# Grouped-query decode with wo loaded in 32 KB rows and turned on VectorE

## The chip, the cores and the metric

The kernel runs on one core of one Trainium2 chip. A core has TensorE (PE, with its weight loads shown as PEld), VectorE (DVE), ScalarE (ACT), GpSimd (POOL), SyncE (SP) and sixteen DMA engines, which all run at once and wait for each other by semaphores. The metric is the device time of one execution in microseconds, as the median of several runs; lower is better.

## The reference

Two layers follow each other twice, with the same weights and the same caches both times: grouped-query attention over a cache, and a gated dense layer. There are 4 rows of 512 numbers (B = 4, one token each), 32 query heads, 8 key and value heads, 4096 cached positions, 128 numbers a head. All inputs are bfloat16.

```python
def A(x, k_cache, v_cache, wq, wo):                  # wq 512x4096, wo 4096x512
    q = (x @ wq).reshape(B, 1, 32, 128).transpose(0, 2, 1, 3)
    k = repeat(k_cache, 4, axis=1)                   # cache: 4 x 8 x 4096 x 128
    v = repeat(v_cache, 4, axis=1)
    p = softmax(einsum("bhqd,bhkd->bhqk", q, k) * 128 ** -0.5)
    o = einsum("bhqk,bhkd->bhqd", p, v)
    return o.transpose(0, 2, 1, 3).reshape(B, 1, 4096) @ wo

def F(x, w_gate, w_up, w_down):                      # 512x1792, 512x1792, 1792x512
    return (gelu(x @ w_gate) * (x @ w_up)) @ w_down

x = x + A(layernorm(x), ...)
x = x + F(layernorm(x), ...)
x = x + A(layernorm(x), ...)
x = x + F(layernorm(x), ...)
```

The K cache is 32 MiB, the V cache 32 MiB. wq and wo are 4 MiB each, the three dense weights 1.75 MiB each.

## The kernel before

The kernel takes the four rows of x one after the other. For each row b it does the first attention (L = 0), the dense layer, and the second attention (L = 1). K of a row is loaded once and used by both attentions; V is loaded for both, since it doesn't stay. The second dense layer is done once for all four rows at the end.

**Memory.** `KV` has 12 places of 8 KB per partition, each for one head of K or of V (1 MB); a head of V in the second attention often comes as two halves of 512 KB, with rows of 4 KB. `wq_sb`, `wo_sb`, `wg_sb`, `wu_sb` and `wd_sb` hold the weights all the time; the room of `wq_sb` is given to four heads of V at the very end. In `wo_sb` (128 partitions, 32 heads, 512 columns) partition d holds, for each query head, row d of that head's part of wo.

**Steps of an attention.** K comes in with positions on partitions and has to be turned: for six heads of eight VectorE does so in place, in blocks of 32x32 words of 32 bits (`turn`, L366, two instructions of 1024 words a head); for two heads PE and ScalarE do (`kturn` L373, `kcopy` L379). The scores (`scores`, L415) of four heads gather in one bank `S_ps`. VectorE takes the maximum (L421) and makes the bias (L429 to L432), ScalarE the exponential (L438), VectorE turns P in blocks (L447), PE swaps the blocks (L455), ScalarE copies the result (L463). Then come P times V (`values`, L485, 32 matmuls a head), the scaling by the sum (`oscale`, L493), and the output projection with wo (`proj`, L613; `proj_last`, L623, with `half_out` L632 and `half_sum` L639 before it). For L = 0 the projection has four parts by key and value heads: 0 to 3, 4 and 5, 6, and 7. `addback` (L646, L647) adds the result to x. The dense layer is `up` (L655), `ffturn` (L662), the gelu (L678 to L707) and `down` (L715). The next query is made by L538 to L605 and L392.

**Order of the work.** Nothing is scheduled at run time. A planner (`Plan`) knows each step as a node with an engine, a duration and what it depends on. `Plan.run` walks through an imagined execution and gives out the steps one after another; the instructions are issued in this order, engine by engine, and wait for each other by semaphores. Where two steps of one engine could go, the one with the longer way to the end goes first; `LEAD` adds some microseconds to that length by kind of step, and `PATIENCE` says how long an engine may be held back for a more pressing step. Loads stand in one fixed list (`pl.load`) and are all issued by SP in that order (x alone by ScalarE); a load of K or V waits for a place of `KV` whose last reader is done. The second figure of `pl.load` is its cost for the planner, in KB per partition.

`Plan.warm` then finds holes of PE and fills them with matmuls whose result is not used (`spin`, L1004), which keep PE busy; `WARM` and `FILL` set how many.

The list begins with x, wq, the eight heads of K of row 0, the first half of wo (16 query heads, 2 MB), the eight heads of V, the second half of wo, w_gate, w_up, w_down in two halves, then K and V of row 1. Each half of wo comes as 128 partitions times 16 rows of 1 KB (`ld_wo`, L795). A projection of L = 0 waits for the half of wo that holds its heads (`parts`).

Of the kernel before, what the change touches and what calls it, by code (L numbers as in the profile page):

```python
# [10 lines left out]
I32 = mybir.dt.int32  # L11
# [3 lines left out]
P = 128  # L15
# [15 lines left out]
DMA_FETCH = 1.5  # L31
DMA_LEAD = 4.0

PATIENCE = (0.5, 1.5, 0.7)
LEAD = {"tn1": -3, "val0": 1, "sc10": -2, "chain": 2, "sc11": -6, "sm00": 1, "os0": -6, "op": -2, "sm01": 11, "sm10": 10, "qx1": 4, "other": 5, "sc00": 2, "sm11": 8, "os1": -4, "tn0": -2, "sc01": 1}
EARLY = {("pt", 1): 60.0, ("su", 1): 60.0}
WINDOW = 3.413
WARM = 0.45
FILL = 0.7
SPIN = 0.22  # L40
STREAM = {"sc": 0.85, "qm": 0.85, "up": 0.75, "up2": 0.75, "kt": 0.21, "pw": 0.16, "qp": 0.11, "qn": 0.05,
          "su": 0.02, "lnm": 0.03, "xt": 0.1, "ys": 0.2, "dn": 0.38, "dn2": 0.38}
# [2 lines left out]
def stage(n):  # L45

    if isinstance(n, str):
        return "end"
    if n[0] in ("val", "va", "vd", "vf", "os"):
        return f"{'os' if n[0] == 'os' else 'val'}{n[2]}"  # L50
    if n[0] == "sc" or n[0] in ("mx", "bi", "ex", "pt", "pw", "pc", "su", "rc"):
        return f"{'sc' if n[0] == 'sc' else 'sm'}{n[2]}{n[3]}"
    if n[0] in ("tn", "kt", "kc"):
        return f"{'tn' if n[0] == 'tn' else 'kt'}{n[2] // 4}"
    if n[0] in ("op", "yo", "ys", "oa"):
        return "op"
    if n[0] in ("qs", "qp", "qx"):
        return f"qx{n[2]}"
    if n[0] in ("lnq", "lnm", "lnc", "lnv", "lnr", "up", "ft", "ga", "gb", "gy", "gc", "zz", "dn", "da", "qm", "qe",
                "qt", "qn", "qc", "qk"):  # L60
        return "chain"
    return "other"


class Plan:
# [7 lines left out]
    def add(self, name, eng, dur, deps, emit, acq=(), rel=(), soft=(), ins=0):  # L73
        assert name not in self.nodes, name
        self.nodes[name] = dict(eng=eng, dur=dur, deps=[d for d in deps if d is not None],
                                emit=emit, acq=acq, rel=rel, soft=list(soft), ins=ins)
        return name
# [9 lines left out]
    def levels(self):  # L87
# [6 lines left out]
        for first in nodes:  # L94
            stack = [first]
            while stack:
# [8 lines left out]
                level[m] = own + max([level[a] for a in after[m]], default=0.0)  # L105
        return {n: v + LEAD.get(stage(n), 0.0) + EARLY.get(n[:1] + n[2:3], 0.0) for n, v in level.items()}

    def run(self, slots, extra=()):
# [16 lines left out]
        while len(order) < len(nodes):  # L125
# [12 lines left out]
            for eng, c in cand.items():  # L138
                c.sort()
                s, lv, n = c[0]  # L140
                for s2, lv2, n2 in c[1:]:
                    if s2 > s + min(PATIENCE[0] * nodes[n]["dur"], PATIENCE[1]):
                        break
                    if lv2 < lv - PATIENCE[2] and s2 - c[0][0] < PATIENCE[1]:
                        s, lv, n = s2, lv2, n2
# [37 lines left out]
            else:  # L183
                ready.discard(n)
                e = s + v["dur"]
                if v["eng"] == "PE":
                    gap = min(s - free.get("PE", 0.0), 1.2 if n[0] == "val" else 99.0)
                    done += 2 * int(max(0.0, FILL * gap - 0.2) / SPIN)
                    while done > edge:
# [25 lines left out]
    def warm(self, places):  # L215
# [3 lines left out]
        for n, _ in self.order:  # L219
# [5 lines left out]
            if place:  # L225
                busy = sum(t * min(1.0, (y - (z - WINDOW)) / (y - x)) for x, y, t in past if y > z - WINDOW)
                most = 1.2 if n[0] == "val" else z - a
                k = max(int(min(most, max(0.0, FILL * (z - a) - 0.2)) / SPIN),
                        min(int(max(0.0, z - a - 0.05) / SPIN), int(max(0.0, WARM * WINDOW - busy) / SPIN + 1.0)))
                if k:  # L230
# [10 lines left out]
def kernel(  # L241
# [13 lines left out]
    nc = tc.nc  # L255
# [17 lines left out]
    wo_sb = wts.tile([P, Hq, D], BF16, name="wo_sb")  # L273
# [10 lines left out]
    def keep(shape, dt, name):  # L284
# [41 lines left out]
                            op=ALU.add)  # L326
# [410 lines left out]
    pl = Plan()  # L737
    add = pl.add

    def plain(dst, src, pat):  # L740
        return lambda pick: nc.sync.dma_start(out=dst, in_=src.rearrange(pat, q=P))  # L741

    def groups(b, L):

        g = [[0, 1, 2, 3], [4, 5], [6], [7]]
        if L:
            g = [[7], [6, 5, 4], [3, 2, 1, 0]] if b < B - 1 else [[0], [1, 2, 3], [7], [4, 5], [6]]
        return g
# [4 lines left out]
    def loads_k(b):  # L753
        for j in range(8):
            soft = []
            if b and j >= 3:
                soft = [("sc", b - 1, 1, 0 if j < 7 else 1, 1)]
            elif b:
                soft = [("val", b - 2, 1, 2 - j, 1) if b > 1 else ("val", 0, 0, 4 + j, 1)]
            pl.load(("k", b, j), 8, ld_head(("k", b, j), A_k_cache[b, j]), [("sc", b, 1, j // 4, 1)],  # L760
                    soft=soft)

    def loads_v(b, L):
        heads = [j for j in sum(groups(b, L), []) if not (L and j in HELD[b])]
        for i, j in enumerate(heads):
            halves = (b, L, j) in HALVES
            held = L == 0 and j in HELD[b]
            if L == 0:
                if j >= 4:
                    soft = [("val", b, 0, j - 4, 1)]  # L770
                elif b and j == 3 and HELD[b - 1]:
                    soft = [("val", b - 1, 1, HELD[b - 1][0], 1)]
                else:
                    soft = [("sc", b - 1, 1, 1, 1)] if b else []
                soft = [soft, soft]
            elif b == B - 1:
                soft = [[("sc", b, 1, 0, 1)]] * 2
            elif i < 3:
                soft = [[("val", b + 1, 0, 4 + i, 1)]] * 2
            else:  # L780
                soft = [[("val", b, 1, heads[i - 3], m)] for m in range(2)]
            src = A_v_cache[b, j]
            name = ("v", b, L, j)
            rd = [[("val", b, L, j, m)] + ([("val", b, 1, j, m)] if held else []) for m in range(2)]
            if halves:
                for m in range(2):
                    pl.load(name + (m,), 4.1, ld_part(name, m, src), rd[m], soft=soft[m], half=True)
            else:
                pl.load(name, 8, ld_head(name, src), rd[0] + rd[1], soft=soft[1])
# [1 line left out]
    def ld_x(pick):  # L791
        nc.scalar.dma_start(out=xr[0:16], in_=A_x.rearrange("b s (t n) -> (b s t) n", t=4))

    def ld_wo(n):
        return lambda pick: nc.sync.dma_start(  # L795
            out=wo_sb[:, 16 * n:16 * n + 16],
            in_=A_wo[2048 * n:2048 * n + 2048].rearrange("(h p) n -> p h n", p=P))

    def ld_wd(k):
        return lambda pick: nc.sync.dma_start(  # L800
# [2 lines left out]
    pl.load("x", 0.5, ld_x, None)  # L803
    pl.load("wq", 32, plain(wq_sb[:], A_wq, "(q c) n -> q c n"), None)
    loads_k(0)
    pl.load(("wo", 0), 20.5, ld_wo(0), None)
    loads_v(0, 0)
    pl.load(("wo", 1), 20.5, ld_wo(1), None)
    pl.load("wg", 14, plain(wg_sb[:], B_w_gate, "(q c) n -> q c n"), None)
    pl.load("wu", 14, plain(wu_sb[:], B_w_up, "(q c) n -> q c n"), None)  # L810
    for k in range(2):
# [32 lines left out]
    def spread_q(b, L, z, after):  # L844
        a = add(("qs", b, L, z), "DVE", 0.26, [after, ("qp", b, L, 0) if z else None],
                qsplit(z, 0 if L else b))
        p = add(("qp", b, L, z), "PE", 0.2, [a], qrep(z), acq=("T1",), ins=8)
        add(("qx", b, L, z), "DVE", 0.4, [p, ("sc", b, L, 0, 1) if z else
                                          (("sc", b, 0, 1, 1) if L else ("sc", b - 1, 1, 1, 1) if b else None)],
            expand(z), rel=("T1",))  # L850
        return a
# [16 lines left out]
    qproj("i", a, al, B, rrow, r, 0)  # L868
    pl.nodes[("qm", "i", 0)]["deps"].append("wq")

    def parts(b, L):

        g = groups(b, L)
        if L == 0:
            return [(h, [("os", b, 0, i), ("wo", h[0] // 4)]) for i, h in enumerate(g)]
        return [(h, [("os", b, 1, i)]) for i, h in enumerate(g)]

    def outproj(tag, b, L, bs, nb, after):
        pre, p = None, parts(b, L)
        whole = len(p) - (1 if L else 2)  # L880
        for k, (heads, deps) in enumerate(p[:whole]):
            pre = add(tag + (k,), "PE", 0.21 * len(heads) + 0.15, deps + [pre] + after,
                      proj(OT[L], nb, heads, k == 0, k == whole - 1), ins=8 * len(heads))
        free = [("val", b, 0, j, 1) for j in range(4)]
        for m in range(2):
            pre = add(("yo",) + tag + (m,), "ACT", 0.4, [pre] + free, half_out(m))
            pre = add(("ys",) + tag + (m,), "PE", 0.5, [pre], half_sum(m, nb), ins=8)
            free = []
        for k, (heads, deps) in enumerate(p[whole:]):
            pre = add(tag + (whole + k,), "PE", 0.21 * len(heads) + 0.15, deps + [pre] + after,  # L890
                      proj_last(OT[L], nb, heads, k == len(p) - whole - 1), ins=32 * len(heads))
        return add(("oa",) + tag, "DVE", 0.52, [pre], addback(bs, nb, 1))

    dense_end = None
    for b in range(B):
        bs = slice(b, b + 1)
        for L in range(2):
            if L == 0:
                if b:
                    q = spread_q(b, 0, 0, ("qx", b - 1, 1, 1))  # L900
# [41 lines left out]
            if L == 0:  # L942
                a = outproj(("op", b), b, 0, bs, 1, [dense_end] + was2)
                a = ln(("f", b), a, bs, 1, rs[:, 0:1])
                g = [None, None]
# [34 lines left out]
    c = add("rowz", "DVE", 0.1, [("os", B - 1, 1, i) for i in range(len(groups(B - 1, 1)))], rows_clear)  # L980
    c = add("rows", "DVE", 0.7, [a, c], rows)
    a = ln("f2", a, al, B, rs)
    g = [None, None]
# [68 lines left out]
```

## Time and profile before

| | |
|---|---|
| median of 3 runs | 292.16 us (292.12 to 294.27) |
| profiled execution | 291.89 us, of which the span of the profile is 290.1 us |
| bytes read from HBM | 111.42 MB |
| loads of K, and of V | 32 of 1 MB; 38 of 1 MB and 46 of 512 KB |
| loads of wo | 2 of 2 MB |
| granted PE clock | 0.998 |

The page gives each engine's busy time, cuts the span into 40 slices with a digit for the busy tenths of each, sums up the DMA queues, and follows back the chain of work that ended last. The windows give the same figures for stretches that one chooses: the length, then for each engine busy microseconds and the number of instructions, the granted clock, the share of time in which the sixteen DMA engines had packets under way (over 1 where packets overlap), and GB/s. In the timeline, a row has the start, the duration, the engine, the line, the operation with what it writes and reads, and in brackets how long the engine had stood idle before and what ended that. SPq are the instructions with which SP issues loads; their long durations are waits for room.

### The profile page before, as it was taken

To read this page: it belongs to the slowest core of one execution; us is meant where nothing else is said; L and a number is where in the kernel's file an instruction comes from. 1 tells how busy PE (TensorE), PEld (TensorE's weight loads), DVE (VectorE), ACT (ScalarE), POOL (GpSimd) and SP (SyncE) were. 2 spreads that over 40 slices of the span, in tenths; PEclk is the share of its full clock that TensorE was granted. 3 is DMA by queue.
4 is the path that set the end of the run, shared out by engine and by line. 5 is a ranking of instruction groups with operands and counts; after the bars stand their busy time and mean duration, and the time that the engine had idled before them with its cause. 6 is when DMAs were issued, how large, how long until landed. Compare 5 with 4: busy or idle time off the path is not lost.

```text
span 290.1 us, 9733 instructions
## 1 busy us (share of the span) xinstructions
PE 236.3 (81%) x4419; PEld 138.3 (48%) x4419; DVE 133.5 (46%) x380; ACT 74.5 (26%) x167; POOL 0.7 (0%) x6
## 2 busy tenths in 40 slices
PE   4988887878687888798888698879977889897794
PEld 1433454443233565455434465554445655565552
DVE  4149911002289942052389721343998213444034
ACT  1020751001023852101224731000338321113010
POOL 0000000000000000000000000000000000000000
PEclk9999999999999999999999999999999999999999
DMA  7999999999999999999999999999999999999910
GB/s 312 412 421 419 376 405 416 414 371 426 415 407 395 419 421 417 402 407 406 393 417 416 425 416 411 405 407 390 413 422 416 408 387 403 396 382 420 411 47 1
DMA packets 21657, 112.04 MB, mean 386 GB/s; under 512 B 2032, under 2 KB 6128, under 8 KB 12272
## 3 DMA queue, kind: packets, MB, share of 16 engines
q1 hardware_dynamic: 21568, 111.42, 95.3%
q8 instruction: 34, 0.56, 0.8%
q14 instruction: 7, 0.06, 0.0%
q10 hardware_dynamic: 48, 0.01, 0.0%
HBM read 111.42 MB, written 0.00 MB: 384 GB/s over the span
## 4 chain that ended last, share of the span: by engine, by line
DMA 62%; PE 16%; SPq 11%; DVE 7%; issue 2%; ACT 1%; DVEq 0%
DMA KV<-in_A_v_cache_dram 43%; DMA KV<-in_A_k_cache_dram 8%; SPq L351 7%; PE O_ps L485 7%; DMA wd_sb<-in_B_w_down_dram 6%; DMA wq_sb<-in_A_v_cache_dram 5%; SPq L741 3%; PE S_ps L415 3%; DVE KV L366 2%; PE R_ps L715 1%; PE R_ps L538 1%; DVE PA L662 1%; PE S_ps L1004 1%; PE R_ps L655 1%; DVE sm L421 1%
## 5 line engine op out<-in xcount | busy, mean ns | idle before, releaser
L485 PE MATMUL O_ps<-PA,KV 128*128 128x56 bf16 x1920 | 66.3, 188 | 20.8 <-DMA KV<-in_A_v_cache_dram 17.3
L485 PEld LDWEIGHTS <-KV 128*128 128x128 bf16 x1920 | 57.6, 97 | 40.8 <-DMA KV<-in_A_v_cache_dram 32.4
L1004 PE MATMUL S_ps<-iden_b 128*128 128x512 bf16 x226 | 67.7, 401 | 3.6 <-DVE iden_b L321 3.6
L366 DVE STREAM_TRANSPOSE KV<-KV 128x1024 int32<-128x1024 int32 x48 | 56.5, 1214 | 0.6 <-DMA KV<-in_A_k_cache_dram 0.4
L379 ACT ACTIVATE KV<-R_ps 128x512 bf16<-128x512 f32 x64 | 34.9, 595 | 28.0 <-PE R_ps L373 27.9
L415 PE MATMUL S_ps<-KV,PA 128*32 128x512 bf16 x384 | 35.3, 394 | 2.1 <-DVE KV L366 1.3
L1004 PEld LDWEIGHTS <-iden_b 128*128 128x128 bf16 x227 | 21.9, 107 | 27.6 <-issue 11.7
L373 PE MATMUL R_ps<-iden_b,KV 128*128 128x128 bf16 x256 | 22.1, 219 | 6.3 <-ACT KV L379 3.1
L421 DVE TENSOR_REDUCE sm<-S_ps 128x1 f32<-128x512 f32 x16 | 10.8, 677 | 27.4 <-PE S_ps L415 27.4
L373 PEld LDWEIGHTS <-KV 128*128 128x128 bf16 x256 | 15.8, 97 | 14.8 <-issue 10.2
L415 PEld LDWEIGHTS <-PA 128*32 128x32 bf16 x384 | 11.4, 94 | 13.2 <-issue 4.4
L493 DVE TENSOR_TENSOR OT<-O_ps,XS 128x4 bf16<-128x4 f32 (+1 forms) x12 | 2.0, 164 | 32.9 <-PE O_ps L485 32.9
L415 PE MATMUL S_ps<-KV,QN 128*32 128x512 bf16 x128 | 16.8, 381 | 0.2 <-ACT KV L379 0.2
L438 ACT ACTIVATE PA<-S_ps,sm 128x512 bf16<-128x512 f32 x16 | 11.7, 732 | 20.4 <-DVE sm L432 17.6
L632 ACT ACTIVATE PA<-R_ps 128x256 f32<-128x256 f32 x10 | 3.8, 384 | 46.2 <-PE R_ps L613 41.1
L529 ACT ACTIVATE sm<-sm 128x1 f32<-128x1 f32 (+1 forms) x10 | 2.0, 203 | 52.6 <-DVE sm L522 52.6
L493 DVE TENSOR_TENSOR OT<-O_ps,rdk 128x16 bf16<-128x16 f32 (+3 forms) x18 | 3.1, 170 | 26.7 <-PE O_ps L485 26.7
L463 ACT ACTIVATE PA<-T_ps 128x512 bf16<-128x512 f32 x16 | 9.6, 597 | 13.0 <-PE T_ps L455 11.8
L556 DVE STREAM_TRANSPOSE PA<-PA 128x256 int32<-128x256 int32 x10 | 4.4, 437 | 14.9 <-ACT PA L551 14.2
L613 PE MATMUL R_ps<-wo_sb,OT 128*1 128x512 bf16 (+1 forms) x124 | 8.7, 378 | 2.6 <-DMA wo_sb<-in_A_wo_dram 1.4
L646 DVE STREAM_TRANSPOSE PA<-R_ps 128x128 f32<-128x128 f32 x9 | 2.9, 317 | 16.5 <-PE R_ps L623 10.2
L447 DVE STREAM_TRANSPOSE PA<-PA 128x256 int32<-128x256 int32 x16 | 7.0, 434 | 7.5 <-ACT PA L438 7.5
(92 smaller groups left out, 173.9 us busy)
## 6 DMA issues: line engine op xcount, KB each, us to landing
KV<-in_A_v_cache_dram SPq DMA_DIRECT2D x34, 1024.0 KB, 15.0
KV<-in_A_k_cache_dram SPq DMA_DIRECT2D x32, 1024.0 KB, 13.5
KV<-in_A_v_cache_dram SPq DMA_DIRECT2D x46, 512.0 KB, 7.0
wq_sb<-in_A_wq_dram SPq DMA_DIRECT2D x1, 4096.0 KB, 12.2
wo_sb<-in_A_wo_dram SPq DMA_DIRECT2D x2, 2048.0 KB, 19.5
wq_sb<-in_A_v_cache_dram SPq DMA_DIRECT2D x4, 1024.0 KB
wg_sb<-in_B_w_gate_dram SPq DMA_DIRECT2D x1, 1792.0 KB
wu_sb<-in_B_w_up_dram SPq DMA_DIRECT2D x1, 1792.0 KB
```

What stands on the lines that cost most here:

```text
L351: nc.sync.dma_start(out=where[name], in_=src.rearrange("(p c) d -> p (c d)", p=P))
L366: nc.vector.transpose(out=w, in_=w)
L373: nc.tensor.matmul(R_ps[k % 2][:, P * u:P * u + P], lhsT=where[name][:, at:at + P], rhs=iden_b[:], start=True, stop=True)
L379: nc.scalar.activation(out=where[name][:, 512 * k:512 * k + 512], in_=R_ps[k % 2][:], func=ACT.Copy)
L415: nc.tensor.matmul(S_ps[z][32 * t:32 * t + 32], lhsT=w, rhs=k, start=(m == 0 and x == 0), stop=(m == 1 and x == 3))
L421: nc.vector.tensor_reduce(out=cms[:, z:z + 1], in_=S_ps[z][:].rearrange("p c r -> p (c r)"), axis=AX.X, op=ALU.max)
L438: nc.scalar.activation(out=PW[L][z].rearrange("p (a r e) -> p a r e", a=8, e=2), in_=S_ps[z][:].rearrange("p (a e) r -> p a r e", e=2), fu ...
L463: nc.scalar.activation(out=PW[L][z], in_=T_ps[z][:].rearrange("p t x -> p (t x)"), func=ACT.Copy)
L485: nc.tensor.matmul(Ov[L][:, j], lhsT=vw[:, c, :], rhs=w[:, c // 2, :, c % 2].unsqueeze(1).broadcast_to([P, WIDE, 4]), start=(m == 0 and c ...
L613: nc.tensor.matmul(R_ps[0][32 * i:32 * i + nb, :], lhsT=src[:, 4 * j + i, 0:nb], rhs=wo_sb[:, 4 * j + i, :], start=(first and j == heads[0 ...
L741: return lambda pick: nc.sync.dma_start(out=dst, in_=src.rearrange(pat, q=P))
L1004: nc.tensor.matmul(sinks[place].rearrange("p (a n) -> p a n", a=4), lhsT=iden_b[:], rhs=every, start=True, stop=True)
```

## The change

wo is now loaded whole, in four DMAs, right behind K of row 0 and ahead of V. DMA q fills partitions 32q to 32q + 31: partition 32q + h gets, for query head h, the rows 32q to 32q + 31 of that head's part of wo, which lie behind each other in HBM as 32 KB. So each partition holds one query head's quarter, where the projection wants one row of every head. Eight new steps on VectorE (`wo_turn`) set this right in place: each takes 32 words of 32 bits (64 columns of wo) of the 32 rows of a partition, and turns the 32x32 blocks of heads by rows. After them `wo_sb` holds what it held before. Each of the eight waits for all four DMAs, and every projection of L = 0 waits for all eight.

The planner's figures change with it: the cost of a load of wo, and `PATIENCE`, `LEAD`, `WARM` and `FILL`. Nothing else is edited; the order in which the planner gives out the steps of each engine changes with the figures.

```diff
-PATIENCE = (0.5, 1.5, 0.7)
-LEAD = {"tn1": -3, "val0": 1, "sc10": -2, "chain": 2, "sc11": -6, "sm00": 1, "os0": -6, "op": -2, "sm01": 11, "sm10": 10, "qx1": 4, "other": 5, "sc00": 2, "sm11": 8, "os1": -4, "tn0": -2, "sc01": 1}
+PATIENCE = (0.5, 1.5, 0.4)
+LEAD = {"tn1": -3, "val0": 1, "sc10": -2, "chain": 2, "sc11": -6, "sm00": 1, "os0": -7, "op": 1, "sm01": 7, "sm10": 10, "qx1": 4, "other": 2, "sc00": 2, "sm11": 6, "os1": -4, "tn0": -2, "sc01": 1, "end": -1}
...
-WARM = 0.45
-FILL = 0.7
+WARM = 0.5
+FILL = 0.8
...
-    def ld_wo(n):
+    def ld_wo(q):
         return lambda pick: nc.sync.dma_start(
-            out=wo_sb[:, 16 * n:16 * n + 16],
-            in_=A_wo[2048 * n:2048 * n + 2048].rearrange("(h p) n -> p h n", p=P))
+            out=wo_sb[32 * q:32 * q + 32].rearrange("p c n -> p (c n)"),
+            in_=A_wo.rearrange("(h q c) n -> q h (c n)", q=4, c=32)[q])
+
+    def wo_turn(k):
+        def emit():
+            w = wo_sb[:].rearrange("p c n -> p (c n)").bitcast(I32).rearrange("p (c n) -> p n c", c=32)
+            w = w[:, 32 * k:32 * k + 32]
+            nc.vector.transpose(out=w, in_=w)
+        return emit
...
     loads_k(0)
-    pl.load(("wo", 0), 20.5, ld_wo(0), None)
+    for q in range(4):
+        pl.load(("wo", q), 7.8, ld_wo(q), None)
     loads_v(0, 0)
-    pl.load(("wo", 1), 20.5, ld_wo(1), None)
...
+    wo_ready = [add(("wt", k), "DVE", 1.25, [("wo", q) for q in range(4)], wo_turn(k)) for k in range(8)]
+
     def parts(b, L):
 
         g = groups(b, L)
         if L == 0:
-            return [(h, [("os", b, 0, i), ("wo", h[0] // 4)]) for i, h in enumerate(g)]
+            return [(h, [("os", b, 0, i)] + wo_ready) for i, h in enumerate(g)]
```

## The prediction

> **What bounds the kernel now.** I read the page first: engines, slices, queues, chain.
>
> ```profile
> span 290.1 us, 9733 instructions
> PE 236.3 (81%) x4419; PEld 138.3 (48%) x4419; DVE 133.5 (46%) x380; ACT 74.5 (26%) x167; POOL 0.7 (0%) x6
> DMA  7999999999999999999999999999999999999910
> DMA packets 21657, 112.04 MB, mean 386 GB/s; under 512 B 2032, under 2 KB 6128, under 8 KB 12272
> q1 hardware_dynamic: 21568, 111.42, 95.3%
> DMA 62%; PE 16%; SPq 11%; DVE 7%; issue 2%; ACT 1%; DVEq 0%
> ```
>
> No compute engine is full. The queue that loads K, V and weights has packets under way for 95.3% of all engine time, its row of digits falls only in the last two slices, and DMA holds 62% of the chain. So the kernel is a stream of 111 MB followed by a tail. What the stream does not do at full rate is the time that can be had; the windows show where that is.
>
> ```profile
> core 0: us, PE busy (x) PEld busy (x) DVE busy (x) ACT busy (x) POOL busy (x), PEclk, DMA share, GB/s
> 2.00:12.00 10.00, 8.29 (x35) 3.03 (x36) 3.85 (x23) 0.43 (x3) 0.00 (x0) 1.00 0.92 389
> 14.00:30.00 16.00, 13.87 (x127) 5.74 (x126) 11.61 (x16) 1.63 (x4) 0.00 (x0) 1.00 1.01 421
> 30.00:40.00 10.00, 8.24 (x109) 4.99 (x101) 5.82 (x12) 8.68 (x17) 0.00 (x0) 1.00 1.06 375
> 40.00:56.00 16.00, 13.76 (x269) 8.23 (x267) 2.16 (x8) 2.46 (x5) 0.00 (x0) 1.00 1.01 419
> 56.00:66.00 10.00, 6.96 (x94) 3.67 (x94) 0.49 (x3) 0.00 (x0) 0.00 (x0) 1.00 1.08 381
> ...
> 86.00:88.00 2.00, 1.94 (x29) 0.83 (x22) 1.90 (x7) 0.18 (x1) 0.00 (x0) 1.00 0.81 324
> ...
> 254.00:256.00 2.00, 1.54 (x36) 0.85 (x28) 1.11 (x3) 0.60 (x1) 0.00 (x0) 1.00 1.00 342
> 256.00:258.00 2.00, 2.00 (x33) 0.81 (x32) 0.00 (x0) 0.00 (x0) 0.00 (x0) 1.00 1.01 350
> ...
> 274.00:276.00 2.00, 1.42 (x40) 0.99 (x37) 0.17 (x1) 0.00 (x0) 0.00 (x0) 1.00 0.97 389
> 276.00:278.00 2.00, 1.95 (x53) 1.21 (x50) 0.18 (x1) 0.03 (x1) 0.00 (x0) 1.00 0.28 104
> ```
>
> The last column is the rate. Rows of 8 KB run at 419 to 421. Two stretches of 10 us run at 375 and 381 although the engines are more than full (1.06, 1.08). SP's order of issue says that these are the halves of wo: each is issued between K and V, or between V and the dense weights.
>
> ```profile
> 15.39 0.38 SPq L795 DMA_DIRECT2D wo_sb<-in_A_wo_dram  x1
> 17.88 33.57 SPq L351 DMA_DIRECT2D KV<-in_A_v_cache_dram  x8
> 51.50 0.43 SPq L795 DMA_DIRECT2D wo_sb<-in_A_wo_dram  x1
> 51.98 8.13 SPq L741 DMA_DIRECT2D wg_sb<-in_B_w_gate_dram  x1
> ```
>
> wo is 4 MiB (4.19 MB) in rows of 1 KB, so 4096 of the 6128 packets under 2 KB. Data stops about 276.5; 13.6 us of PE and VectorE work follow, which this edit leaves as it is.
>
> **The change, part by part.**
>
> *wo's rows.* 4096 rows of 1 KB become 128 rows of 32 KB, 32 in each of four DMAs. At 420 GB/s the bytes of the two slow stretches would have taken 10 × (375 + 381) / 420 = 18.0 us, not 20.0. Lost to the short rows: 2.0 us; wo therefore costs 4.19 / 0.42 + 2.0 = 12.0 us of stream now. The nearest row for 32 KB rows is wq, which is all of the first stretch: 389 GB/s, with the start-up in it. At 389 wo would take 10.8 us and the gain is 1.2; at 420 it is 2.0. I take 1.8, nearer to 420, because the share of 0.92 in that row says that engines idled there. All this holds if a DMA onto 32 partitions is as fast as one onto 128. Every large row of this trace has 128, so that is not shown; the other side of it is the third rival.
>
> [...]
>
> *Order of the loads.* The second half of wo moves from behind V to ahead of it, past eight V loads on SP's queue; four issues replace two, some 0.4 us each, on a queue that is waiting anyway (V's eight issues last 33.57 us). Bytes ahead of wd are the same. The first V lands later by half of wo's new time less half the gain, about 5.0 − 0.9 = 4.1 us, and everything from wg on lands 1.8 us earlier. A V that comes later does not empty the stream: V4 to V7 need places that V0 to V3 free, and each V0 to V3 still has the others queued behind it.
>
> *Eight turns on VectorE.* Each is a 128x1024 int32 transpose, as K's are, but reads and writes words 1 KB apart.
>
> ```profile
> L366 DVE STREAM_TRANSPOSE KV<-KV 128x1024 int32<-128x1024 int32 x48 | 56.5, 1214 | 0.6 <-DMA KV<-in_A_k_cache_dram 0.4
> L447 DVE STREAM_TRANSPOSE PA<-PA 128x256 int32<-128x256 int32 x16 | 7.0, 434 | 7.5 <-ACT PA L438 7.5
> ...
> L728 DVE STREAM_TRANSPOSE PA<-PA x1: 408/408/408, 281.0 to 281.0; 128x128 f32<-128x128 f32 x1
> ...
> 43.59 0.16 DVE L432 SCALAR_TENSOR_TENSOR sm<-sm 128x4 f32<-128x4 f32 x1
> ...
> 44.66 0.45 DVE L447 STREAM_TRANSPOSE PA<-PA 128x256 int32<-128x256 int32 x1 [0.91 <-ACT PA L438]
> 45.12 0.26 DVE L474 RECIPROCAL XS<-S_ps 128x16 f32<-128x16 f32 x1
> 51.13 0.17 DVE L493 TENSOR_TENSOR OT<-O_ps,rdk 128x16 bf16<-128x16 f32 x1 [5.75 <-PE O_ps L485]
> ```
>
> Contiguous, 1024 words cost 1.21 us. The bound above: the slope of the two contiguous sizes is (1214 − 434) / 768 = 1.016 ns a word, so 128 would take 304 ns; L728, which writes 16 B apart, takes 408. That 0.81 ns a word makes 1024 take 2.04 us. I take 1.21, the same size and form. Eight then cost 9.7 us (at most 16.3).
>
> They stand in VectorE's order after the second softmax bias: one ahead of L447, seven behind L474. The first waits for all four quarters, and behind it queue L447, then on PE the swap of P and the first V matmul. wo lands about 10.0 + 1.5 us after K, and K's last bytes come near 31.5 (12.58 MB of wq and K from about 1 us on at 389 to 421), so near 43: when L432 is done at 43.75. The wait is about nothing. The seven then run from about 45.8 to 54.3, in the hole of 5.75 us that waited for V's matmuls and the 4.1 by which V3 is later; L493 is due at 51.13 + 4.1 = 55.2. So they are covered. At 2.04 us they would end at 60.1, and PE, which has the first part of the output projection ahead of V4's matmuls, stands until then. Does that reach the end?
>
> ```profile
> 65.96 0.60 PE L613 MATMUL R_ps<-wo_sb,OT 128*1 128x512 bf16 x8 [1.37 <-DMA wo_sb<-in_A_wo_dram]
> ...
> 74.54 0.93 PE L655 MATMUL R_ps<-wu_sb,xn 128*1 128x448 bf16 x16 [1.45 <-DMA wu_sb<-in_B_w_up_dram]
> ...
> 78.90 0.56 PE L715 MATMUL R_ps<-wd_sb,PA 128*1 128x128 bf16 x28 [0.52 <-DMA wd_sb<-in_B_w_down_dram]
> ...
> 86.42 3.08 SPq L351 DMA_DIRECT2D KV<-in_A_k_cache_dram x4
> ```
>
> The dense layers of the first row wait for wu at 74.54 and wd at 78.90, not for the projection. With 1.8 off, wu comes at 72.7; a projection that ends by 70 is not late, which L493 by about 63 allows. That is 2.5 us a turn, over both bounds. The 1.37 that the projection waited for wo is no gain either: wu is next late.
>
> *The next K loads.* After wd come four K loads without waiting; the other four are issued at 86.42, when scores that hang on wd's matmul free their places, and the stream runs short at 86 to 88 (324 against 420: 2 × 0.23 = 0.5 us). Loads and chain both move 1.8 with wd, so the hole stays.
>
> *Leads fitted anew.* They reorder PE by some matmul groups, VectorE by a reciprocal or two per row, and add 16 idle-filling matmuls of 243; SP's order of loads beyond the first row is unchanged. PE is at 81% beside a full stream, so I cost them at 0. Bounds: the slow places that a different order could close or widen are 0.5 us at 86 and 2 × (1 − 342/420) + 2 × (1 − 350/420) = 0.7 at 254 to 258, so ±1.2.
>
> *Sum:* −1.8 (rows) + 0 (order) + 0 (turns) + 0 (leads) = −1.8. The profiled execution took 291.89 us (span 290.1 and 1.8 around it), 0.27 under the median of 292.16. I take the change off the median: **290.4**.
>
> **The rivals.**
>
> *More comes.* The rows' whole 2.0 and the leads' 1.2: 292.16 − 3.2 = 289.0. For it: the two slow places hang on orders that did change. Against: the chain through wd sets the first.
>
> *Nothing comes.* 32 KB rows at 128 KB pitch over 32 partitions run no better than the 375 of now, or the leads give back 1.2 to 1.8: 291.2 to 293. For it: wq, at 389, is the one example of such rows.
>
> *Slower: a quarter of the partitions takes half the rate.* All sixteen engines share the 420 GB/s of a 128-partition load. If the rows of one quarter can be written over half of the paths only, each DMA runs at 210: wo takes 4.19 / 0.21 = 20.0 us in place of 12.0, and a full stream hands the +8.0 to the end: 300.2. It decides from 4.19 / 12.0 = 350 GB/s down; overlap of neighbouring quarters gives values between, +1 to +5. For it: nothing here shows a large load of 32 partitions at full rate. Against: neighbouring quarters are queued together, and the engines could work on different ones. [...]
>
> **How the numbers follow.** Forecast, 289.6 to 291.4: 0.45. More: 0.13. Nothing: 0.12. Slower: 0.30 (0.24 near 300, 0.06 between). A measurement of this kernel tells about 1%, 2.9 us, from no change: faster is below 289.2, slower above 295.1. Faster: most of "more" 0.11, and 0.01 of the rest, 0.12. Slower: 0.24 and half of the partial cases, 0.28. Same: 0.60. The forecast's own range is 289.6 to 291.4; the range on record must take in most of the slow case, 288.9 to 300.5, which holds 0.45 + 0.12 + 0.06 + 0.16 + 0.03 = 0.82.
>
> **What would show it.** Right: the stretch of wo, about 31 to 42, at 400 or more; no second dip at 56 to 66; V's first matmul near 47; turns of about 1.2 us, ended before L493; wd's matmul near 77; the whole row of loads 1.8 us earlier to the end. Wrong: wo's stretch at 210 for 20 us, with the first turn blocked till it ends; turns over 2.5 us; or rates as predicted with a hole that has grown at 86 or 254.

## The result, and the profile after

The changed kernel takes 306.49 us (median of 4 runs, 305.69 to 307.64) against 292.33 us of the kernel before beside it: a ratio of 1.0468, with a 95% interval of 1.042 to 1.0517, so 14 us slower. The forecast was 290.4, with a range up to 300.5. The profiled execution has a span of 304.5 us, 14.4 more than before. The ratios here and below are taken over the fast runs alone: a run more than 1.5% above the fastest of its kernel is left out.

The page of the changed kernel, in the same order as before: span, DMA and rate in 40 slices (7.6 us each), chain by engine, the group of the new turns, and the issues of wo.

```profile
span 304.5 us, 9781 instructions
DMA  8899998999997699999999999999999999999900
GB/s 341 383 425 417 293 209 194 407 383 414 421 417 292 253 419 424 413 406 406 406 400 423 418 420 414 409 406 373 393 423 417 418 419 405 400 410 415 400 35 1
DMA 55%; PE 25%; DVE 13%; issue 3%; ACT 2%; SPq 1%; DVEq 0%; ACTq 0%
L803 DVE STREAM_TRANSPOSE wo_sb<-wo_sb 128x1024 int32<-128x1024 int32 x8 | 16.6, 2151 | 10.7 <-DMA wo_sb<-in_A_wo_dram 10.7
wo_sb<-in_A_wo_dram SPq DMA_DIRECT2D x4, 1024.0 KB, 28.6
```

The row of rates of the kernel before, in slices of 7.3 us:

```profile
GB/s 312 412 421 419 376 405 416 414 371 426 415 407 395 419 421 417 402 407 406 393 417 416 425 416 411 405 407 390 413 422 416 408 387 403 396 382 420 411 47 1
```

Two places in the rate are new, and beyond them the row is much as before: slices 5 to 7 (293, 209, 194) and slices 13 and 14 (292, 253). The windows of the changed kernel show them closer, beside one window of undisturbed loads; the last three columns are granted PE clock, DMA share and GB/s.

```profile
core 0: us, PE busy (x) PEld busy (x) DVE busy (x) ACT busy (x) POOL busy (x), PEclk, DMA share, GB/s
14.00:30.00 16.00, 14.23 (x134) 5.89 (x132) 12.94 (x19) 2.06 (x5) 0.00 (x0) 1.00 1.02 423
...
32.00:42.00 10.00, 7.41 (x84) 4.14 (x82) 2.51 (x4) 6.89 (x14) 0.00 (x0) 0.84 1.13 242
42.00:52.00 10.00, 3.68 (x28) 1.55 (x27) 1.28 (x5) 1.13 (x3) 0.00 (x0) 0.84 0.89 183
...
53.50:60.00 6.50, 1.88 (x45) 1.68 (x45) 4.41 (x4) 0.60 (x1) 0.00 (x0) 0.50 1.01 407
86.00:92.00 6.00, 5.58 (x73) 2.20 (x68) 2.75 (x11) 0.34 (x2) 0.00 (x0) 1.00 1.00 415
92.00:106.00 14.00, 12.55 (x205) 5.87 (x193) 10.73 (x26) 3.26 (x9) 0.00 (x0) 1.00 0.67 260
```

The first place is wo itself. Its 4.19 MB run at 242 and 183 GB/s for some 20 us (the two windows together move 4.25 MB), where 420 GB/s would take 10. In the first of the two windows the engines are more than full (1.13): packets are under way all the time, and fewer bytes come through. The second place is another thing: between 92 and 106 the share is 0.67. The stream stands there because its next loads have no place to go: SP's longest wait of this part, 17.1 us, ends with the scores (L415).

What it costs in all can be summed over the stretch of both kernels that holds wo, here from the windows before and after:

```profile
8.00:56.00 48.00, 41.87 (x511) 21.37 (x512) 20.52 (x41) 13.19 (x28) 0.00 (x0) 1.00 1.01 409
```
```profile
8.00:56.00 48.00, 32.93 (x284) 15.38 (x284) 20.03 (x39) 12.50 (x27) 0.00 (x0) 0.89 1.00 326
```

Against 420, this stretch lost 48 × 94 / 420 = 10.7 us after and 1.3 before, where the second half of wo lost 0.9 more outside it: 2.2. The rate of wo is worth 8.5 us. The hole at 92 to 106 lost 14 × 160 / 420 = 5.3 against 0.5 before: 4.8 us. Together 13.3 of the 14.4 us of span.

Why the second place stands empty is read from VectorE's timeline after, then PE's, then SP's.

```profile
55.59 2.17 DVE L803 STREAM_TRANSPOSE wo_sb<-wo_sb 128x1024 int32<-128x1024 int32 x1 [10.70 <-DMA wo_sb<-in_A_wo_dram]
57.67 0.40 DVE L447 STREAM_TRANSPOSE PA<-PA 128x256 int32<-128x256 int32 x1
...
58.14 14.45 DVE L803 STREAM_TRANSPOSE wo_sb<-wo_sb 128x1024 int32<-128x1024 int32 x7
72.49 0.13 DVE L493 TENSOR_TENSOR OT<-O_ps,rdk 128x16 bf16<-128x16 f32 x1
```
```profile
58.12 0.62 PE L455 MATMUL T_ps<-PA,iden_b 128*32 128x128 bf16 x16 [11.69 <-DVE PA L447]
...
72.68 1.88 PE L613 MATMUL R_ps<-wo_sb,OT 128*1 128x512 bf16 x16 [5.81 <-DVE OT L493]
```
```profile
77.27 2.05 SPq L351 DMA_DIRECT2D KV<-in_A_k_cache_dram  x2
...
100.47 2.16 SPq L351 DMA_DIRECT2D KV<-in_A_k_cache_dram  x4
```

The first turn waits 10.7 us for the last quarter, and behind it in VectorE's order stands the turn of P (L447), behind that on PE the swap of P (idle for 11.69) and all matmuls with V. (This wait itself costs little, as the run without the turns shows below: V, which now lands behind wo, is late as well.) Seven more turns of 2.15 us follow. The scaling L493 stands behind them, the projection behind it, and V4's matmuls behind the projection. The dense layers come that much later, and the K loads that were issued at 86.42 wait until 100.47.

So there are two terms: the rate of wo, and the length and lateness of the turns. The experiments are about these. All times below are compared by the ratio to the kernel before, run beside them.

### The profile page after: what moved, and what is told of

It is laid out like the page before. It is cut to its first block, busy times and chain, and to the rows that moved or that the text cites. A ratio compares the mean times of both kernels' runs of the same rounds, so it can differ in the third digit from the quotient of the medians.

```text
span 304.5 us, 9781 instructions
## 1 busy us (share of the span) xinstructions
PE 241.8 (79%) x4435; PEld 141.4 (46%) x4435; DVE 149.0 (49%) x388; ACT 74.2 (24%) x167; POOL 0.7 (0%) x6
## 4 chain that ended last, share of the span: by engine, by line
DMA 55%; PE 25%; DVE 13%; issue 3%; ACT 2%; SPq 1%; DVEq 0%; ACTq 0%
DMA KV<-in_A_v_cache_dram 35%; DMA wo_sb<-in_A_wo_dram 10%; DMA KV<-in_A_k_cache_dram 10%; PE O_ps L485 9%; DVE wo_sb L803 5%; PE S_ps L415 4%; PE S_ps L1013 3%; PE R_ps L613 2%; PE R_ps L655 1%; ACT PA L438 1%; DVE KV L366 1%; DVE sm L421 1%; DVE PA L662 1%; PE R_ps L538 1%; PE R_ps L715 1%
## 5 line engine op out<-in xcount | busy, mean ns | idle before, releaser
L485 PE MATMUL O_ps<-PA,KV 128*128 128x56 bf16 x1920 | 67.9, 189 | 16.5 <-DMA KV<-in_A_v_cache_dram 11.5
L485 PEld LDWEIGHTS <-KV 128*128 128x128 bf16 x1920 | 59.5, 97 | 37.6 <-DMA KV<-in_A_v_cache_dram 25.7
L1013 PE MATMUL S_ps<-iden_b 128*128 128x512 bf16 x237 | 69.4, 399 | 3.6 <-DVE iden_b L321 3.6
L415 PE MATMUL S_ps<-KV,PA 128*32 128x512 bf16 x384 | 36.1, 399 | 1.1 <-DVE KV L366 0.7
L1013 PEld LDWEIGHTS <-iden_b 128*128 128x128 bf16 x243 | 23.0, 106 | 27.7 <-issue 10.0
L373 PEld LDWEIGHTS <-KV 128*128 128x128 bf16 x256 | 16.1, 98 | 15.6 <-issue 9.8
L803 DVE STREAM_TRANSPOSE wo_sb<-wo_sb 128x1024 int32<-128x1024 int32 x8 | 16.6, 2151 | 10.7 <-DMA wo_sb<-in_A_wo_dram 10.7
L493 DVE TENSOR_TENSOR OT<-O_ps,XS 128x4 bf16<-128x4 f32 (+1 forms) x12 | 2.0, 164 | 33.2 <-PE O_ps L485 33.2
L415 PE MATMUL S_ps<-KV,QN 128*32 128x512 bf16 x128 | 17.2, 396 | 0.0
L415 PEld LDWEIGHTS <-PA 128*32 128x32 bf16 x384 | 11.9, 95 | 11.3 <-issue 3.4
L455 PE MATMUL T_ps<-PA,iden_b 128*32 128x128 bf16 x256 | 6.7, 226 | 11.8 <-DVE PA L447 11.7
L613 PE MATMUL R_ps<-wo_sb,OT 128*1 128x512 bf16 (+1 forms) x124 | 9.6, 409 | 7.0 <-DVE OT L493 6.8
L493 DVE TENSOR_TENSOR OT<-O_ps,rdk 128x16 bf16<-128x16 f32 (+3 forms) x18 | 3.0, 168 | 19.5 <-PE O_ps L485 19.4
L556 DVE STREAM_TRANSPOSE PA<-PA 128x256 int32<-128x256 int32 x10 | 4.4, 437 | 13.5 <-ACT PA L551 12.9
```

The source lines that it names most:

```text
L373: nc.tensor.matmul(R_ps[k % 2][:, P * u:P * u + P], lhsT=where[name][:, at:at + P], rhs=iden_b[:], start=True, stop=True)
L415: nc.tensor.matmul(S_ps[z][32 * t:32 * t + 32], lhsT=w, rhs=k, start=(m == 0 and x == 0), stop=(m == 1 and x == 3))
L455: nc.tensor.matmul(T_ps[z][32 * i:32 * i + 32, t].rearrange("p (a m x) -> p a m x", a=8, m=2), lhsT=iden_b[:, 32 * t:32 * t + 32], rhs=w[: ...
L485: nc.tensor.matmul(Ov[L][:, j], lhsT=vw[:, c, :], rhs=w[:, c // 2, :, c % 2].unsqueeze(1).broadcast_to([P, WIDE, 4]), start=(m == 0 and c ...
L613: nc.tensor.matmul(R_ps[0][32 * i:32 * i + nb, :], lhsT=src[:, 4 * j + i, 0:nb], rhs=wo_sb[:, 4 * j + i, :], start=(first and j == heads[0 ...
L803: nc.vector.transpose(out=w, in_=w)
```

## The experiments

**Is it the partitions or the source?** The changed rows differ from all others in two ways: 32 partitions in a row, and 32 KB pieces 128 KB apart in HBM. The first run spreads each DMA over all partitions and leaves the source as it is.

```diff
-            out=wo_sb[32 * q:32 * q + 32].rearrange("p c n -> p (c n)"),
+            out=wo_sb[:].rearrange("p c n -> p (c n)")[q:P:4],
```

> The changed kernel, but DMA q of wo writes partitions q, q+4, ..., q+124 in place of 32q to 32q+31: the same four DMAs of 32 rows of 32 KB from the same places of HBM, the same turns. What wo_sb holds after the turns is then not wo in its order, so the projections are not the reference's. Theory A (a DMA onto one quarter of the partitions writes at half rate): wo runs at 400 GB/s or more, is landed by about 44, the turns end near 62 at 2.15 us each, and the time falls by 8.7 for the rate, 2.0 for the rows and most of the second hole: 290 to 294 us. Theory B (rows of 32 KB at a pitch of 128 KB in HBM are slow to read): wo stays near 200 GB/s and the time near 306.

295.52 us, ratio 1.0108 (1.005 to 1.0167). Windows, then VectorE's timeline of this run:

```profile
30.00:42.00 12.00, 10.36 (x117) 5.72 (x117) 5.28 (x11) 9.19 (x19) 0.00 (x0) 1.00 1.00 427
...
84.00:92.00 8.00, 6.93 (x98) 3.10 (x97) 6.87 (x15) 2.65 (x7) 0.00 (x0) 1.00 0.36 119
```
```profile
44.33 2.17 DVE L803 STREAM_TRANSPOSE wo_sb<-wo_sb 128x1024 int32<-128x1024 int32 x1 [1.86 <-DMA wo_sb<-in_A_wo_dram]
...
61.21 0.15 DVE L493 TENSOR_TENSOR OT<-O_ps,rdk 128x16 bf16<-128x16 f32 x1
...
72.60 0.32 DVE L646 STREAM_TRANSPOSE PA<-R_ps 128x128 f32<-128x128 f32 x1 [0.57 <-PE R_ps L623]
82.30 0.32 DVE L646 STREAM_TRANSPOSE PA<-R_ps 128x128 f32<-128x128 f32 x1 [1.64 <-PE R_ps L715]
```

Only the destination partitions differ from the changed kernel, and wo runs at 427 GB/s: no loss to short rows is left. The source reads well. The time missed its expectation by 1.5 us on the upper side, because the hole at 84 to 92 stayed (119 GB/s: 5.7 us lost), although wo was on time and the stream behind it full (420 GB/s from 72 to 84).

The opposite edit keeps the partitions and makes the source one piece:

```diff
-            in_=A_wo.rearrange("(h q c) n -> q h (c n)", q=4, c=32)[q])
+            in_=A_wo.rearrange("(q h c) n -> q h (c n)", q=4, c=32)[q])
```

> The changed kernel, but DMA q of wo reads 1 MB that lies in one piece in HBM, still in 32 rows of 32 KB onto partitions 32q to 32q+31; wo_sb then holds other rows of wo, so the projections are not the reference's. Theory A (destination quarter): nothing changes, wo near 200 GB/s, 305 to 308 us. Theory B (source pitch): wo at 400, 290 to 296 us.

306.93 us, ratio 1.0488 (1.0412 to 1.0563), with this window:

```profile
31.50:53.50 22.00, 11.63 (x113) 5.92 (x114) 4.21 (x10) 8.68 (x17) 0.00 (x0) 0.79 1.01 222
```

The changed kernel has 222 in the same stretch. Nothing is gained, so the source pitch falls as a cause.

**Quarter or half?** The next run has each DMA span 64 partitions, every second one of a half.

```diff
-            out=wo_sb[32 * q:32 * q + 32].rearrange("p c n -> p (c n)"),
+            out=wo_sb[:].rearrange("p c n -> p (c n)")[64 * (q // 2) + q % 2:64 * (q // 2) + 64:2],
```

> DMA q of wo writes every second partition of one half: 0, 2, ..., 62 for q = 0, then 1, 3, ..., 63, then the same in 64 to 127; the rest as changed, and the projections are not the reference's. If what counts is the half of the partitions that a DMA stays in, wo keeps 200 GB/s and the time is 304 to 308, although each DMA spans twice as many partitions. If it is the quarter (32 partitions in a row), wo comes to 400 and the time to 294 to 296, as in the spread run.

307.7 us, ratio 1.0513 (1.0474 to 1.0552):

```profile
31.50:53.50 22.00, 11.79 (x123) 6.22 (x122) 6.24 (x16) 10.33 (x21) 0.00 (x0) 0.91 1.01 220
```

Twice the span within one half, and the same rate, where the same rows over both halves ran at 427: the quarter is not what counts, and a limit in each half of the partitions fits all four runs (427 GB/s over both halves; 222, 222 and 220 within one). One rival is left: the run at 427 GB/s also has its partitions four apart, the other three one or two apart, and no run has them four apart within one half.

**Can the two halves be written at once?** Two runs: the quarters in the order 0, 2, 1, 3, and quarters 2 and 3 issued by ScalarE on its own queue.

```diff
-    for q in range(4):
+    for q in (0, 2, 1, 3):
         pl.load(("wo", q), 7.8, ld_wo(q), None)
```

> The changed kernel with the quarters of wo issued in the order 0, 2, 1, 3. If each DMA by itself is held to half rate, because all engines work on the same quarter, nothing changes: wo near 200 GB/s, 305 to 308 us. If quarters 0 and 1 obstruct each other, as do 2 and 3, and the engines work on neighbouring DMAs at once, the alternation brings wo to 300 GB/s or more and the time to 295 to 302.

305.38 us, ratio 1.0395 (1.0305 to 1.0484), with wo at

```profile
32.00:52.00 20.00, 9.72 (x108) 5.02 (x107) 3.76 (x9) 7.86 (x16) 0.00 (x0) 0.92 0.98 211
```

```diff
-        return lambda pick: nc.sync.dma_start(
+        return lambda pick: (nc.scalar if q > 1 else nc.sync).dma_start(
             out=wo_sb[32 * q:32 * q + 32].rearrange("p c n -> p (c n)"),
```

> The changed kernel with quarters 2 and 3 of wo issued by ScalarE, on its own queue, beside quarters 0 and 1 on SP's. If the two queues let the engines write to both halves of the partitions at once, wo comes near 400 GB/s, though partly beside K: 293 to 297 us, as in the spread run. If the engines stay in step and all write the same half at a time, wo keeps about 200 GB/s, K is delayed by the share that moves ahead, and the time is 304 to 309.

309.1 us, ratio 1.0515 (1.0443 to 1.0586). ScalarE's two quarters are issued at 9.36, so they run beside K, and the stretch 8 to 56 has

```profile
8.00:56.00 48.00, 36.81 (x281) 16.06 (x281) 20.13 (x38) 12.05 (x26) 0.00 (x0) 0.86 1.00 320
```

against 326 of the changed kernel. The other order changed nothing in the rate (211, against 212 in the same stretch of the changed kernel), and its ratio is within the noise of the changed kernel's. The second queue gained nothing either, but this run does not put the two halves side by side. ScalarE's quarters landed 10.2 us after their issue, the last near 23, and SP issued the other two only from 29.71 on. What it shows is that K, which goes to all partitions, is held up too while a quarter of wo is loaded beside it: from 16 to 24 both together run at 219 and 168 GB/s (8 to 28 has 297 in the mean, as 9.4 of the 15.4 MB of the stretch above are moved after 28; the changed kernel has 414 there), and from 28 to 40 K alone at 422 to 424. Whether two loads into the two halves would run together if they were under way at once is not shown. Why a load within one half runs at half the rate isn't shown either: the trace has no engine numbers for its packets.

**The turns.** Left out of the changed kernel:

```diff
-    wo_ready = [add(("wt", k), "DVE", 1.25, [("wo", q) for q in range(4)], wo_turn(k)) for k in range(8)]
+    wo_ready = [("wo", q) for q in range(4)]
```

> The changed kernel without the eight turns: the projection waits for the four DMAs alone and takes wo_sb unturned, so its result is not the reference's. Theory A: wo stays at 200 GB/s until about 55, V lands as before, the first projection comes near 60 to 62 in place of 72.7, the loads of K after it are issued 8 to 10 us earlier, and the second hole (5 to 6 us lost between 87 and 106) closes: 300 to 302 us. Rival (the second hole is the work of the leads fitted anew, not of late turns): 305 to 307.

302.95 us, ratio 1.0352 (1.0304 to 1.04). The stretch 86 to 106 of this run has a share of 0.99:

```profile
86.00:106.00 20.00, 16.52 (x257) 8.25 (x258) 15.99 (x38) 6.34 (x15) 0.00 (x0) 1.00 0.99 401
```

The hole is gone with the turns, though the leads are the fitted ones. By the ratios it gave 3.4 us of the 4.8 that the stream had lost, slightly less than expected, and the first projection came at 66.11, not at 60 to 62. The wait of the first turn was not what cost the time: here P is turned and swapped by 47, and the first matmul with V still starts only at 57.33, after a wait of 10.02 us for V's load, against 58.67 with the turns. The turns cost time by the seven (14.45 us) that stand ahead of L493: in the changed kernel PE is through with V3's matmuls at 66.65, and the projection waits 5.81 us for L493. Together with the spread rows:

> Partitions q, q+4, ... for DMA q of wo, as before in this study, and the eight turns left out; the projections then take wo in another order than the reference's. Theory A with late turns as the cause of the hole that stayed (84 to 91 in the spread run, about 6 us in which the stream stood): with wo at 420 GB/s and no turns the first projection comes near 55, the hole shrinks to what the kernel before has (0.5 us), and the time is 290 to 292 us. Rival (wo ahead of V, which puts every V 4 us later, or the leads make the hole): 294 to 296 as with the turns.

291.84 us, ratio 0.9959 (0.9933 to 0.9984). As the first theory has it: with neither of the two terms, the kernel is a little faster than before (0.5 to 2.0 us).

**Why are the turns long?** The same eight instructions on words that lie behind each other, once at full rate and once in the changed kernel:

```diff
-            w = wo_sb[:].rearrange("p c n -> p (c n)").bitcast(I32).rearrange("p (c n) -> p n c", c=32)
-            w = w[:, 32 * k:32 * k + 32]
+            w = wo_sb[:].rearrange("p c n -> p (c n)").bitcast(I32)[:, 1024 * k:1024 * k + 1024]
```

> Partitions q, q+4, ... for DMA q of wo, and the eight turns on 1024 words that lie behind each other, in place of words 1 KB apart; wo_sb then does not hold wo in its order, so the projections are not the reference's. This is the case that the forecast summed: wo at full rate and turns of the size of K's. If the stride makes the turns long, they take 1.21 us each in place of 2.15, end near 55, and the time is 290 to 292.5 us. If they stay at 2.15, the stride is not the cause and the time is 295 to 296.

291.66 us, ratio 0.9945 (0.9909 to 0.9981). First what the trace has on wo_sb's turns in this run (shortest, median and longest in ns, first and last start), then the window of the hole, then VectorE's timeline, each in a fence of its own:

```profile
L802 DVE STREAM_TRANSPOSE wo_sb<-wo_sb x8: 1186/1202/1245, 44.4 to 52.8; 128x1024 int32<-128x1024 int32 x8
```
```profile
84.00:92.00 8.00, 6.73 (x106) 3.28 (x98) 7.48 (x21) 2.05 (x6) 0.00 (x0) 1.00 0.94 347
```
```profile
54.94 0.17 DVE L493 TENSOR_TENSOR OT<-O_ps,rdk 128x16 bf16<-128x16 f32 x1 [0.98 <-PE O_ps L485]
...
65.65 0.32 DVE L646 STREAM_TRANSPOSE PA<-R_ps 128x128 f32<-128x128 f32 x1 [0.57 <-PE R_ps L623]
77.39 0.32 DVE L646 STREAM_TRANSPOSE PA<-R_ps 128x128 f32<-128x128 f32 x1 [2.24 <-PE R_ps L715]
```

1.20 us a turn, ended before L493, which now waits for V's matmuls. The stream loses 1.4 us in this window, where the kernel before loses 0.7. This is the kernel that the forecast summed.

> The changed kernel, with quarters of the partitions as it has them, but the eight turns on 1024 words that lie behind each other; wo_sb then does not hold wo in its order. The half rate and the turns are taken for two separate terms: wo still near 200 GB/s until 53, turns of 1.21 us, ended near 66 in place of 72.5, and the time falls by 3 to 4, as it did at full rate: 302 to 304 us. If the second hole has little to do with the turns once wo is late: 305.5 to 307.

302.48 us, ratio 1.0322 (1.0281 to 1.0362): by the ratios 4.3 us off, much as at full rate (1.0108 to 0.9945, 4.8), so the two terms add up as separate ones. The stretch 86 to 106 runs at 391 GB/s. For the side of the stride:

```diff
+            f = w[:, 1024 * k:1024 * k + 1024].rearrange("p (n c) -> p n c", c=32)
...
-            nc.vector.transpose(out=w, in_=w)
+            nc.vector.transpose(out=f, in_=w)
```

> Partitions q, q+4, ... for DMA q, and turns that read words 1 KB apart but write them behind each other, so wo_sb holds no wo; the projections are not the reference's. A look at the length of a turn: with both sides strided it was 2.15 us, with neither 1.21 is expected. If the read costs it: 2.1 here; if the write: 1.2 to 1.3; if each side costs half: near 1.7.

One run, 294.72 us, and for a turn:

```profile
L804 DVE STREAM_TRANSPOSE wo_sb<-wo_sb x8: 1872/1906/1953, 44.5 to 58.5; 128x1024 int32<-128x1024 int32 x8
```

Neither side strided 1.20, the read alone 1.91, both 2.15: the read costs 0.71 of the 0.95 us, the write 0.24 on top. None of the three expectations met it. That a strided write alone costs 0.24 wasn't tried. Why the strided read costs more than the strided write isn't shown.

**The planner.** The leads alone, on the kernel before:

> The kernel before with the changed kernel's PATIENCE, LEAD, WARM and FILL and nothing else. Theory A costs the leads at 0 with bounds of 1.2: 291.1 to 293.5 us. Rival (the leads are a part of the loss): 294 us or more.

293.8 us, ratio 1.004 (0.9997 to 1.0084). The median is 0.3 above the expected band; the interval reaches from nothing to 2.5 us. They give no gain here, and a loss of about 1 us is likely but not shown. And the measured costs, told to the planner:

```diff
-        pl.load(("wo", q), 7.8, ld_wo(q), None)
+        pl.load(("wo", q), 16.5, ld_wo(q), None)
...
-    wo_ready = [add(("wt", k), "DVE", 1.25, ...
+    wo_ready = [add(("wt", k), "DVE", 2.15, ...
```

> The changed kernel with what was measured given to the planner: a load of wo costs 16.5 (was 7.8) and a turn 2.15 us (was 1.25). It can put V's matmuls ahead of the projection that waits for the turns. The half rate stays, so wo ends near 53. If the second hole comes of PE standing behind a projection that the planner held for early, it closes as without turns: 302 to 304 us. If the late turns hold the dense layer in any order: 305 to 307.

304.17 us, ratio 1.0379 (1.0326 to 1.0433), by the ratios 2.6 us better than the changed kernel (the two intervals overlap at their ends), and 0.2 above the expected 302 to 304. PE's timeline of this run:

```profile
71.21 1.03 PE L485 MATMUL O_ps<-PA,KV 128*128 128x56 bf16 x32
73.43 1.47 PE L613 MATMUL R_ps<-wo_sb,OT 128*1 128x512 bf16 x24 [1.19 <-DVE OT L493]
```

It now does V4's and V5's matmuls before the projection and then two parts of it at once, though L493 is no earlier (73.22). The stretch 92 to 106 runs at 384 GB/s in place of 260. P, too, is now turned ahead of all eight turns, but the first matmul with V starts at 58.73, no earlier than before, since it waits for V's load. So a part of the second term was PE standing behind a projection that the planner took for early; the half rate stays.

No version that was run and that computes the whole of the reference beats the kernel before.

## Why the prediction was wrong

*What bounds the kernel:* right. Outside of the two places the stream runs as before, and what it lost there came to the end: 13.3 of 14.4 us.

*wo's rows:* the size of the gain was right and the condition under it wrong. The forecast took 32 partitions to be as fast as 128 and named that as not shown. With rows over all partitions the term holds: at 427 GB/s nothing of the 2.0 us is left, and the whole kernel, with turns as short as the forecast took them, came out at a ratio of 0.9945, 1.6 us faster (0.6 to 2.7), where −1.8 was summed. In the changed kernel each DMA stays in one half. This is the step that failed, and it is the third rival: priced at +8.0, and the windows give 8.5. Its rate of 210 was an estimate, half of 420; no row of the kernel before shows a large load onto 32 partitions, and 242 and 183 were measured. I gave it 0.30, on the thought that neighbouring quarters might be worked on at once. With the order 0, 2, 1, 3, where neighbours lie in different halves, the rate was 211, so that thought found no support.

*Eight turns:* mis-sized, and the larger surprise. The value taken was 1.21 us and the bound above 2.04; it is 2.15. The bound came from L728, where only the write is strided; the strided read, which no transpose among the lines shown has in SBUF, costs most.

*"2.5 us a turn, over both bounds":* wrong also at full rate. I let L493 come as late as 63 and the projection end as late as 70. In the spread run L493 came at 61.21, before that limit, and the hole still cost 5.7 us. Both steps between were too short. From the end of the projection to wd's result (the two L646 rows) the spread run needs 82.30 − 72.60 = 9.7 us when it waits for no weight. In the run with short turns the projection ends at 65.65 and wd's result is at 77.39, so the slack was 77.39 − 65.65 − 9.7 = 2.0 us: the projection must end by 67.7, not by 70. And from L493 to that end it took 72.60 − 61.21 = 11.4 us, not 7, since V4's to V7's matmuls, the later parts of the projection and the filling matmuls between them all stand behind its first part. The run with short turns needs 65.65 − 54.94 = 10.7 us for the same stretch, at a granted clock of 1.00, so PE's low clock after its wait (0.50 from 61.4 to 63.4; see below) is the smaller part. The loads of K behind this chain had no slack either: the 0.5 us hole at 86 was the sign of it, and I read it only as "the hole stays". With long turns wd's result came 82.30 − 77.39 = 4.9 us later than with short ones, and the stream lost 5.7 us in place of 1.4.

*The wait of the first turn, "about nothing":* 10.7 us in the changed kernel, 1.9 at full rate. What stood behind it was named rightly (L447, the swap of P, the first V matmul), but little hung on it, since V's load was late as well (57.33 without the turns, 58.67 with them).

*Order of the loads:* right; V later by the time of wo, no harm seen from that by itself (the run with rows spread and no turns has a ratio of 0.9959). *Leads:* 0 with bounds of 1.2; measured +1.2, within −0.1 to +2.5.

*The range:* its top, 300.5, was about the middle of the slow case taken alone. The two terms were treated as exclusive, half rate here and long turns there, while the runs show them to add: short turns take off 4.8 us at full rate and 4.3 at half rate. Half rate at 8.0 and the 4.8 of the hole, on 292.16, sum to 305; the measured 306.49 is 1.5 above that, 0.5 of it by the 8.5 that the windows give for the rate; the rest stays open.

## What to carry to other kernels

Before a load is cut into blocks of partitions, ask which half each block lies in: here DMAs onto 32 partitions four apart ran at full rate (427 GB/s), DMAs onto 32 partitions within one half, in a row or every second one, at half of it (222 and 220), and another order of the four did not mend that (211). An operation moved into a hole must be priced with the strides that it has there (a turn took 2.15 us here, 1.20 without them), and the slack behind it is read from the chain to the next load that waits for a place, not from which weight was waited for. A small hole in a stream that is otherwise full can be the sign that the chain before it has no slack, as the 0.5 us at 86 were here.

## What the runs showed that was not expected

A strided read of SBUF made VectorE's 1024-word transpose 1.6 times as long (1.20 to 1.91 us), a strided write on top of it 0.24 us more.

The granted clock fell in PE's two long waits of the changed kernel: before, it was 1.00 in all windows shown; after, with PE waiting from 46 to 58, it was 0.74 from 48 to 50, stood at 0.50 from 50 to 62, and was 1.00 again from 64 to 66. Sixteen matmuls of the projection took 1.88 us at 72.68, after another wait of 5.81 and at a granted clock of 0.50 (72.7 to 74.6), where the kernel before, whose timeline has this row, took 1.03:

```profile
51.36 1.03 PE L613 MATMUL R_ps<-wo_sb,OT 128*1 128x512 bf16 x16
```

The filling matmuls are placed in holes that the planner foresees; in the two waits above, which it did not foresee, PE had none, its granted clock fell to 0.50, and what came after ran slowly too (32 matmuls with V took 1.67 us at 58.67, and 1.03 at 63.90, near the return to 1.00).
